# A two-layer decode kernel: W2's last blocks loaded over its first, more of head 29 kept, x on ScalarE's queue, and one small load in eight pieces

## The chip, the cores and the metric

The kernel runs on one core of a Trainium2 chip. The metric is device time in microseconds (us), and the time given for a kernel is the median of several executions. A profile is one execution taken by the hardware profiler. Its engines are PE (TensorE), DVE (VectorE), ACT (ScalarE), POOL (GpSimd) and SP (SyncE). Loads are issued by SP or ACT and carried out by sixteen DMA engines.

## The reference

One token passes twice through the same attention block and the same MLP. The cache does not change, so each layer reads all of it: 32 heads of 8192 keys and values of 128 numbers, in float32.

```
def _A_ref(x, k_cache, v_cache, wq, wo):
    q = (x @ wq).reshape(B, Sq, H, Dh).transpose(0, 2, 1, 3)      # H = 32, Dh = 128, D = 640
    scores = einsum("bhqd,bhkd->bhqk", q, k_cache) * (Dh ** -0.5) # Sk = 8192
    o = einsum("bhqk,bhkd->bhqd", softmax(scores), v_cache)
    return o.transpose(0, 2, 1, 3).reshape(B, Sq, H * Dh) @ wo
def _B_ref(x, w1, w2):                                            # Dff = 1728
    return relu(x @ w1) @ w2
x = x + _A_ref(layernorm(x), k_cache, v_cache, wq, wo)
x = x + _B_ref(layernorm(x), w1, w2)
x = x + _A_ref(layernorm(x), k_cache, v_cache, wq, wo)
x = x + _B_ref(layernorm(x), w1, w2)
```

## The kernel before

**Heads.** `attention_and_mlp` (L612) runs once per layer. Layer 1 (L = 0 in the code) takes heads 0 to 31, layer 2 (L = 1) takes them from 31 down to 0. For a head, `scores` (L443) multiplies the keys that lie in SBUF by the query; `row_maxima` and `exponentials` (L458, L461) make the softmax's numerators with DVE and ACT and turn them; `values` (L491) multiplies them by the values; `output` (L507) collects the head's column for the projection with `wo`. The last head of a layer is interleaved with the projection and the MLP (`before_last`, L662).

**The ring.** Keys, values and W2 lie in one large tile, `ring`. Its places are counted in units of 8 columns of all 128 partitions (4096 bytes). The table `UNITS` (L42 to L61) cuts each head into loads; a piece ("k", [(r, c, n)]) is n columns of keys of row r from column c on, a piece ("v", [(b, r, m)]) is a share of the values' block b. A load's pieces lie next to each other in memory, in the order of the table. `pump` (L190) issues loads from the list `todo` on SP's queue as long as the next one finds room, and `release` (L222) gives back a piece's place when TensorE has used it and pumps again. So SP's loads stand in the order of `todo`, and each waits for the reads that free its place.

**What is kept.** From the end of layer 1 some units stay in SBUF for layer 2, which takes these heads first: `DROPPED` (L62) says from which unit on, `KEPT` (L63) how many places they take. Two more pieces of head 30 (432 and 160 columns of keys) are loaded at the change of layers into tiles that layer 1 no longer needs, `mix` and `wct`, by `load_beside` (L210), called at L806 and L845. `pieces_of` (L227) takes the kept pieces of a head first in layer 2.

**W2.** W2's twelve full blocks (80 places each) come in four loads, `W2_RUNS` (L93: blocks 0 to 3, 4 to 7, 8 and 9, 10 and 11), and have 960 places of their own behind the kept ones at the end of layer 1. The loop at L859 reads them in the order 0 to 3, two short blocks that lie elsewhere, 4 to 11.

**Mixing.** At the ninth head of a layer (`where == 8`, L697) ACT loads one head's rows of `wo` (128 x 640) into `mix`; later steps multiply them by W1 beside the attention, so that the last head's output can go to the MLP directly. Just ahead of it on ACT's queue stands a load of Wq (`load_wq`, L239).

**Signals.** Each load signals one of eight semaphores, named DMAHW0 to DMAHW7 in the rows below, in turn over both queues; a load waits until the previous load on its own semaphore has landed. PE stands for TensorE's semaphore.

**The start.** SP issues x (L248), the first Wq (L249) and then the ring's loads.

Of the kernel before, what the change touches and what calls it, by code (L numbers as in the profile page):

```python
# [15 lines left out]
P = 128  # L16
D = 640
# [3 lines left out]
DFF = 1728  # L21
EPS = 1e-5
NB = D // P
HG = 4
# [21 lines left out]
UNITS[29] = [  # L46
    ("k", K_ALL[:1]),
    ("k", K_ALL[1:2]),
    ("k", [(2, 0, 512), (3, 0, 384)]),
    ("v", V_ALL[:1]),  # L50
    ("v", V_ALL[1:2]),
    ("k", [(3, 384, 128)]),
    ("v", V_ALL[2:3]),
    ("v", V_ALL[3:]),
]
UNITS[30] = [
    ("k", [(0, 432, 80), (1, 0, 80)]),
# [1 line left out]
    ("k", [(1, 80, 432)] + K_ALL[2:]),  # L59
] + HALVES[2:]  # L60
UNITS[31] = HALVES[:2] + LAST  # L61
DROPPED = {30: 2}  # L62
KEPT = 3800  # L63
MIX_AT = [12, 16, 20, 24]
AHEAD = 3

# [10 lines left out]
def wide(kind, piece):  # L77

    if kind == "w":
        return D // 8  # L80
    return 4 * piece[2] * (1 if kind == "k" else DH) // 8


def size(unit):
    return sum(wide(kind_of(unit, t), piece) for t, piece in enumerate(unit[1]))
# [4 lines left out]
F_TILES = 3  # L90
# [2 lines left out]
W2_RUNS = [range(0, 4), range(4, 8), range(8, 10), range(10, 12)]  # L93
UNITS["w2"] = [("w", list(run)) for run in W2_RUNS]
W2_ALL = [("w2", i) for i in range(len(W2_RUNS))]
RING = KEPT + 4 * F_TILES * D // 8


@with_exitstack
def decode_kernel(ctx: ExitStack, tc: tile.TileContext, x, kv, wq, wo, w1, w2, w2_rest, out):  # L100
    nc = tc.nc
# [11 lines left out]

    ring = consts.tile([P, 8 * RING], F32, name="ring")
    order = [(h, i) for h in range(H) for i in range(len(UNITS[h]))]
    kept = [u for u in order if u[0] >= min(DROPPED) and u[1] >= DROPPED.get(u[0], 0)]
    assert sum(size(UNITS[h][i]) for h, i in kept) == KEPT
    beside = [(1, u) for u in order if u[0] == 30 and u not in kept]
    todo = []

    def all_of(layer, u):
# [35 lines left out]
    for us, dram in ((order, kv), (W2_ALL, w2)):  # L157
        o = 0
        for u in us:
            n = 8 * P * size(UNITS[u[0]][u[1]])  # L160
# [5 lines left out]
    def place(layer, u, n):  # L166

        step = 512 if n % 512 == 0 else 8
        if layer:
            low, high = 0, RING  # L170
        elif u[0] in range(FULL[0]):
            low, high = 0, 16 * SLOT
        elif u[0] == "w2":
            low, high = KEPT, RING
        else:
            low, high = (3072, KEPT) if n == KEPT - 3072 else (0, 3072)
        at, best = low, None
        for a, m in sorted(live.values()) + [(high, 0)]:
            a = min(a, high)
            for base in (0, KEPT):  # L180
                c = base + -(-max(at - base, 0) // step) * step
                if a - c >= n and (best is None or a - at < best[1]):
                    best = c, a - at
            at = max(at, a + m)
        return None if best is None else best[0]
# [4 lines left out]
    def pump():  # L190
        while todo:
            layer, u, first, last, at = todo[0]
            unit = UNITS[u[0]][u[1]]
            ns = [wide(kind_of(unit, t), piece) for t, piece in enumerate(unit[1])]
            n = sum(ns[first:last])
            if at is None:
                at = place(layer, u, n)
                if at is None:
                    return
            elif not is_free(at, n):  # L200
                return
            todo.pop(0)
            o = 8 * sum(ns[:first])
            nc.sync.dma_start(ring[:, 8 * at : 8 * (at + n)], source[u][:, o : o + 8 * n])
            for t in range(first, last):
                live[layer, u, t] = at, ns[t]
                at_of[layer, u, t] = ring, 8 * at
                at += ns[t]

    def load_beside(where, at, n):  # L210
        layer, u = beside.pop()
        kind, pieces = UNITS[u[0]][u[1]]
        assert 8 * size(UNITS[u[0]][u[1]]) == n
        nc.sync.dma_start(where[:, at : at + n], source[u])
        for t, piece in enumerate(pieces):
            at_of[layer, u, t] = where, at
            at += 8 * wide(kind, piece)

    def key(L, u, t):
        return (0 if u in kept else L), u, t  # L220

    def release(L, u, t):  # L222
        if (L or u not in kept) and at_of[key(L, u, t)][0] is ring:
            del live[key(L, u, t)]
            pump()
# [13 lines left out]
    def load_wq(g, queue):  # L239
        wq_t[g] = wts.tile([P, NB, HG * DH], F32, name="wq_t")  # L240
        queue.dma_start(wq_t[g], wq[g])
# [3 lines left out]
        queue.dma_start(wo_t[g], wo[g])  # L245

    xr = work.tile([P, DR], F32, name="xr", bufs=2)
    nc.sync.dma_start(xr, x)  # L248
    load_wq(0, nc.sync)  # L249
    pump()  # L250
    load_wo(0, nc.sync)
# [24 lines left out]
    mix = consts.tile([P, DFF], F32, name="mix")  # L276
# [335 lines left out]
    def attention_and_mlp(L, xr, s):  # L612
        heads = list(range(H))[:: 1 - 2 * L]
        last = heads[-1]
# [35 lines left out]
        def run_out(k):  # L650

            projected(acc, runs[k], o_cols[k], k == 0, False)
            yield "dve"
            load_wo(groups[k + 1], nc.scalar)
# [26 lines left out]
        def due(h):  # L681

            where = heads.index(h)
            k, j = divmod(where, HG)
            if j == 0:
                o_cols[k] = work.tile([P, HG], F32, name="o_cols", bufs=2)
            if where and j == 0:
                chores.append([run_out(k - 1), "pe"])
            if j == 2 and k + 1 < NG:
                slow.append([queries_of(k + 1), "pe"])  # L690
            if where == H - 2:
                chores.append([first_of_last(), "pe"])
            if L == 0 and where == 4:
                nc.scalar.dma_start(w1_t, w1)
            if L == 0 and where == 7:
                nc.scalar.dma_start(w2_t, w2_rest)
            if where == 8:  # L697
                nc.scalar.dma_start(mix[:, :D], wo[last // HG][:, last % HG])
            if where == 11:
                slow.append([mixing(), "dve"])  # L700
            if where in MIX_AT:
                slow.append([mixing_quarter(MIX_AT.index(where)), "pe"])
# [20 lines left out]
        for where, h in enumerate(heads[:-1]):  # L723
# [36 lines left out]
            k, j = divmod(where, HG)  # L760
# [36 lines left out]
        rows = copied_rows(hd)  # L797
# [4 lines left out]

        xp, ph = mlp_in
        hidden(ph, o, mix, False, True)
        if L == 0:
            load_beside(mix, 0, DFF)  # L806
        pd = ps_m.tile([P, 512], F32, name="pm")
        times_rows(pd, wo_t[last // HG][:, last % HG], o, True, True)
        keep_busy(1, 128)
# [50 lines left out]
        for a, b in enumerate(blocks):  # L860
            if a == 2:
                ss = deviations(x1, s1)
            if a == 8:
                r1 = spread_of_rows(ss)
            rows = 2 * half if b == nb + 1 else P
            if b < nb:
                i = next(i for i, run in enumerate(W2_RUNS) if b in run)
                where = L, ("w2", i), b - W2_RUNS[i][0]
                tile_of, at = at_of[where]
                wt = tile_of[:, at : at + D]  # L870
            else:
                wt = w2_t[:rows, b - nb]
            times_rows(po, wt, hT[:rows, b : b + 1], a == 0, a == len(blocks) - 1)
            if b < nb:
                release(*where)

        x2 = work.tile([P, DR], F32, name="xr", bufs=2)
        s2 = work.tile([P, 1], F32, name="x_s", bufs=2)
# [7 lines left out]
    for L in range(2):  # L886
        xr, s = attention_and_mlp(L, xr, s)
# [80 lines left out]
```

## Time and profile before

| what | value |
|---|---|
| median of three runs (1351.44, 1353.2, 1356.7) | 1353.2 us |
| the profiled execution | 1351.49 us |
| its span, first to last instruction | 1349.7 us |
| moved | 575.17 MB, 426 GB/s over the span |
| SP's queue / ACT's queue | 531.89 MB / 42.44 MB |
| busy: PE / DVE / ACT | 59% / 19% / 4% of the span |

A timeline row reads: start, duration, engine, line, operation, output tile <- inputs, shapes, and in brackets the idle time of that engine before it with what ended it. SPq and ACTq rows are issues of loads. A row of the list of transfers ends with the size of one and the time from issue to landing (where neither stands, it was not recorded). A row of the windows gives start:end, length, the busy time of PE, PE's weight loads, DVE, ACT and POOL with their instruction counts, the clock granted to TensorE, the mean busy share of the sixteen DMA engines and their GB/s. The chain of waits is the work that ended last, followed back: start, length, what.

### The profile page before, as it was taken

Reading aid. Unit: us, or ns where it says so; the run is one execution under the profiler, and the core shown is the slowest. Engines: PE = TensorE matmul, PEld = TensorE weight load, DVE = VectorE, ACT = ScalarE, POOL = GpSimd, SP = SyncE. Lnnn points to the kernel's source line nnn. Section 1 sums busy time; section 2 is a strip of 40 time slices with the busy share of each in tenths; the row PEclk is TensorE's granted clock in tenths of the full one; section 3 lists DMA queues with packets and bytes.
Section 4 is the critical chain, followed back from the end, with each engine's and each line's share of the span. In section 5 each row is a group of like instructions: output and inputs, shape, how many; then the busy total and the mean of one; then the engine's idle time right before and its main releaser. Section 6 shows DMA issues by size and latency. Waiting matters only on the chain.

```text
span 1349.7 us, 13544 instructions
## 1 busy us (share of the span) xinstructions
PE 799.3 (59%) x6048; PEld 270.4 (20%) x6048; DVE 251.4 (19%) x794; ACT 59.2 (4%) x149; POOL 2.9 (0%) x10
## 2 busy tenths in 40 slices
PE   5455555554654655457787754555566554656658
PEld 2011111211211211122242211111121121212214
DVE  1111111221211211122122211122111211111212
ACT  0000000000000000000000000000000000000000
POOL 0000000000000000000000000000000000000000
PEclk8777677878978976788799777797778778777879
DMA  9999999999999999999999999999999999999997
GB/s 392 445 419 437 432 428 441 417 431 436 439 426 432 430 435 422 448 417 420 425 405 423 435 431 432 432 431 436 438 434 424 421 435 443 429 420 438 429 418 322
DMA packets 24977, 575.17 MB, mean 426 GB/s; under 512 B 2772, under 2 KB 2904, under 8 KB 5336
## 3 DMA queue, kind: packets, MB, share of 16 engines
q1 hardware_dynamic: 20312, 531.89, 91.8%
q10 hardware_dynamic: 4608, 42.44, 7.5%
q8 instruction: 47, 0.77, 0.2%
q14 instruction: 10, 0.08, 0.0%
HBM read 574.31 MB, written 0.00 MB: 426 GB/s over the span
## 4 chain that ended last, share of the span: by engine, by line
DMA 65%; PE 27%; DVE 5%; issue 1%; ACT 1%; ACTq 0%; SPq 0%; DVEq 0%
DMA ring<-in_kv 64%; PE ps L448 13%; PE outs L497 8%; DVE h_t L459 2%; PE px L387 1%; DVE pt L477 1%; PE pm L464 1%; ACT p L473 1%; DMA wo_t<-in_wo 1%; DVE p L516 1%; PE acc L419 1%; PE px L419 1%; PE acc L603 0%; PE px L590 0%; DVE pT L479 0%
## 5 line engine op out<-in xcount | busy, mean ns | idle before, releaser
L448 PE MATMUL ps<-ring,spread_q 128*32 128x512 f32 (+2 forms) x2072 | 331.0, 787 | 334.5 <-DMA ring<-in_kv 329.6
L497 PE MATMUL outs<-ring,pT 128*4 128x512 f32 (+1 forms) x2080 | 268.2, 658 | 27.7 <-DVE pT L479 17.4
L448 PEld LDWEIGHTS ps<-ring,spread_q 128*32 128x32 f32 x2072 | 76.9, 138 | 523.2 <-issue 298.4
L459 DVE TENSOR_REDUCE h_t<-ps 128x1 f32<-128x512 f32 x64 | 44.3, 692 | 640.3 <-PE ps L448 640.3
L473 ACT ACTIVATE p<-ps,h_t 128x512 f32<-128x512 f32 x64 | 44.0, 687 | 1226.4 <-DVE h_t L471 1226.4
L497 PEld LDWEIGHTS outs<-ring,pT 128*4 128x4 f32 x2080 | 52.5, 92 | 184.4 <-issue 156.9
L526 PE MATMUL pm<-ones,p 128*128 128x1 f32 x120 | 22.9, 260 | 94.8 <-DVE p L516 94.8
L512 DVE TENSOR_SCALAR p<-outs,ind 128x128 f32<-128x128 f32 x60 | 21.1, 351 | 248.2 <-PE outs L497 248.2
L516 DVE SCALAR_TENSOR_TENSOR p<-outs,ind,p 128x128 f32<-128x128 f32 x180 | 63.1, 351 | 6.4
L477 DVE STREAM_TRANSPOSE pt<-p 128x512 f32<-128x512 f32 x64 | 46.5, 727 | 57.9 <-ACT p L473 57.9
L464 PE MATMUL pm<-row_of,h_t 128*128 128x16 f32 x128 | 25.7, 276 | 49.9 <-DVE h_t L459 49.0
L526 PEld LDWEIGHTS pm<-ones,p 128*128 128x128 f32 x120 | 17.8, 188 | 151.5 <-DVE p L516 149.9
L464 PEld LDWEIGHTS pm<-row_of,h_t 128*128 128x128 f32 x128 | 19.4, 190 | 109.2 <-DVE h_t L459 107.3
L590 PE MATMUL px<-w_t,wct 128*128 128x448 f32 (+1 forms) x80 | 36.6, 573 | 1.1 <-ACT wct L583 1.1
L387 PE MATMUL px<-wq_t,ln_xc 128*32 128x256 f32 x280 | 32.9, 381 | 0.0
L486 PE MATMUL pm<-ind,h_t 128*128 128x1 f32 x128 | 23.4, 252 | 15.3 <-ACT p L473 15.3
L486 PEld LDWEIGHTS pm<-ind,h_t 128*128 128x128 f32 x128 | 23.2, 207 | 34.1 <-ACT p L473 26.6
L419 PE MATMUL acc<-wo_t,o_cols 128*32 128x160 f32 x496 | 22.7, 324 | 0.6 <-DVE o_cols L544 0.6
L527 DVE TENSOR_SCALAR o_cols<-pm,h_t 128x1 f32<-128x1 f32 x60 | 13.1, 218 | 30.6 <-PE pm L526 30.6
L387 PEld LDWEIGHTS px<-wq_t,ln_xc 128*32 128x32 f32 x280 | 15.2, 109 | 12.7 <-issue 1.2
L471 DVE TENSOR_REDUCE h_t<-pm 128x1 f32<-128x16 f32 x64 | 11.2, 175 | 32.4 <-PE pm L464 32.4
L419 PEld LDWEIGHTS acc<-wo_t,o_cols 128*32 128x32 f32 x496 | 15.8, 117 | 4.8 <-issue 2.5
(110 smaller groups left out, 201.2 us busy)
## 6 DMA issues: line engine op xcount, KB each, us to landing
ring<-in_kv SPq DMA_DIRECT2D x20, 4096.0 KB, 34.5
ring<-in_kv SPq DMA_DIRECT2D x38, 2048.0 KB, 29.3
ring<-in_kv SPq DMA_DIRECT2D x11, 6144.0 KB, 38.2
wq_t<-in_wq ACTq DMA_DIRECT2D x14, 1280.0 KB, 23.4
wo_t<-in_wo ACTq DMA_DIRECT2D x14, 1280.0 KB, 23.8
ring<-in_kv SPq DMA_DIRECT2D x15, 1024.0 KB, 16.7
ring<-in_w SPq DMA_DIRECT2D x4, 1280.0 KB, 26.8
w_t<-in_w ACTq DMA_DIRECT2D x1, 4320.0 KB, 47.7
```

The lines of the kernel that those rows point to most:

```text
L387: nc.tensor.matmul(pq[32 * j : 32 * j + 32, :n], xc[:, c : c + 1].to_broadcast([P, 32]), wq_t[g][:, c, j * n : (j + 1) * n], start=(c == 0 ...
L419: nc.tensor.matmul(acc[32 * g : 32 * g + 32, :DR], col.to_broadcast([col.shape[0], 32]), wt[:, g * DR : (g + 1) * DR], start=first, stop=last,
L448: nc.tensor.matmul(hd.ps[32 * g : 32 * g + 32, c : c + n], spread_q[:, 3 - r : 35 - r], tile_of[:, at + g * n : at + (g + 1) * n], start=f ...
L459: nc.vector.tensor_reduce(hd.nm, hd.ps, AX.X, ALU.max, negate=True)
L464: nc.tensor.matmul(pt[:, :16], hd.nm.to_broadcast([P, P]), row_of.rearrange("p g r -> p (g r)"), start=True, stop=True,)
L473: nc.scalar.activation(hd.p, hd.ps, AF.Exp, bias=hd.low, scale=1.0, accum_out=hd.l)
L477: nc.vector.transpose(pt, hd.p)
L486: nc.tensor.matmul(pt[:, :1], hd.l.to_broadcast([P, P]), ind[:, 4:5], start=True, stop=True)
L497: nc.tensor.matmul(hd.out[32 * g : 32 * g + 4, r : r + m].rearrange("p r d -> p (r d)"), hd.pT[:, 4 * i : 4 * i + 4], tile_of[:, v : v + m ...
L516: nc.vector.scalar_tensor_tensor(oc[:, r], hd.out[:, r], ind[:, r : r + 1], oc[:, r - 1], op0=ALU.mult, op1=ALU.add,)
L526: nc.tensor.matmul(pt[:, :1], oc[:, 3], ones, start=True, stop=True)
L590: nc.tensor.matmul(pt[:, :n], wct[:, c], w1_t[:, c, f : f + n], start=(c == 0), stop=(c == NB - 1),)
```

## The change

Four things are changed, with what follows from them.

- W2 gets 800 places instead of 960 in layer 1. Its last load (blocks 10 and 11) is placed over blocks 0 and 1, once these have been read. The load into `wct` now comes ahead of it, and the load into `mix` follows it.
- The 160 places go to 320 columns of keys of head 29, as one more unit at the end of its list. Head 29's keys are cut anew, so that their parts fit the places: seven pieces instead of five.
- x is issued by ACT instead of SP.
- In layer 2 the 128 rows of `wo` for mixing are loaded by eight loads of 96, 11, 6, 5, 4, 3, 2 and 1 rows.

```
 UNITS[29] = [
     ("k", K_ALL[:1]),
     ("k", K_ALL[1:2]),
-    ("k", [(2, 0, 512), (3, 0, 384)]),
+    ("k", [(2, 0, 256)]),
+    ("k", [(2, 256, 256), (3, 128, 64)]),
     ("v", V_ALL[:1]),
     ("v", V_ALL[1:2]),
-    ("k", [(3, 384, 128)]),
+    ("k", [(3, 0, 128)]),
     ("v", V_ALL[2:3]),
     ("v", V_ALL[3:]),
+    ("k", [(3, 192, 320)]),
 ]
...
-DROPPED = {30: 2}
-KEPT = 3800
+MIX_CUT = [[P], [96, 11, 6, 5, 4, 3, 2, 1]]
+DROPPED = {29: 9, 30: 2}
+KEPT = 3960
+W2_PLACES = 800
...
-RING = KEPT + 4 * F_TILES * D // 8
+RING = KEPT + W2_PLACES
...
-    beside = [(1, u) for u in order if u[0] == 30 and u not in kept]
+    apart = {(29, 9): (3800, KEPT), (30, 0): (4464, 4544), (30, 1): (4544, RING), (30, 2): (3072, 3800)}
+    beside = [(1, u) for u in order[::-1] if u[0] == 30 and u not in kept]
...
+        elif u in apart:
+            low, high = apart[u]
         else:
-            low, high = (3072, KEPT) if n == KEPT - 3072 else (0, 3072)
+            low, high = 0, 3072
...
-            for base in (0, KEPT):
+            for base in (0, 3328, KEPT):
...
-    nc.sync.dma_start(xr, x)
+    nc.scalar.dma_start(xr, x)
...
             if where == 8:
-                nc.scalar.dma_start(mix[:, :D], wo[last // HG][:, last % HG])
+                p = 0
+                for rows in MIX_CUT[L]:
+                    part = slice(p, p + rows)
+                    nc.scalar.dma_start(mix[part, :D], wo[last // HG][part, last % HG])
+                    p += rows
...
         hidden(ph, o, mix, False, True)
-        if L == 0:
-            load_beside(mix, 0, DFF)
...
             if b < nb:
                 release(*where)
+            if L == 0 and a == 1:
+                load_beside(mix, 0, DFF)
```

Three places show how instructions moved. The first is TensorE in layer 1: the values of head 28, its output, head 29's scores (ps<-ring), then head 29's softmax and values. Before:

```order
L497 MATMUL outs_118<-ring,pT 4x512 x16
L526 MATMUL pm<-ones,p 128x1
L448 MATMUL ps<-ring,spread_q 32x512 x12
L448 MATMUL ps<-ring,spread_q 32x384 x4
L448 MATMUL ps<-ring,spread_q 32x128 x4
L464 MATMUL pm<-row_of,h_t 128x16
```

Of the change:

```order
L504 MATMUL outs_118<-ring,pT 4x512 x16
L533 MATMUL pm<-ones,p 128x1
L455 MATMUL ps<-ring,spread_q 32x512 x8
L455 MATMUL ps<-ring,spread_q 32x256 x8
L455 MATMUL ps<-ring,spread_q 32x64 x4
L455 MATMUL ps<-ring,spread_q 32x128 x4
L455 MATMUL ps<-ring,spread_q 32x320 x4
L471 MATMUL pm<-row_of,h_t 128x16
```

The last piece of the scores was the 128 columns that are loaded between the values; now it is the 320 columns, loaded after all of head 29's values.

The second place is SP's queue at the change of layers, with the semaphores that each load waits for; in_w is W2, the loads into mix and wct are head 30's keys, and the ring's loads behind them are head 29's for layer 2. Before:

```order
L204 DMA ring<-in_w 128x2560 [waits DMAHW1_49]
L204 DMA ring<-in_w 128x2560 [waits DMAHW2_49]
L204 DMA ring<-in_w 128x1280 [waits DMAHW3_49]
L204 DMA ring<-in_w 128x1280 [waits DMAHW4_49]
L214 DMA mix<-in_kv 128x1728 [waits DVE_49,DMAHW5_49,PE_49,Activation_49]
L214 DMA wct<-in_kv 128x640 [waits DVE_49,DMAHW6_49,PE_49,Activation_49]
L204 DMA ring<-in_kv 128x2048 [waits DMAHW7_49,DMAHW1_49,PE_49]
```

Of the change:

```order
L211 DMA ring<-in_w 128x2560 [waits DMAHW3_49]
L211 DMA ring<-in_w 128x2560 [waits DMAHW4_49,PE_49]
L211 DMA ring<-in_w 128x1280 [waits DMAHW5_49,PE_49]
L221 DMA wct<-in_kv 128x640 [waits DVE_49,DMAHW6_49,PE_49,Activation_49]
L211 DMA ring<-in_w 128x1280 [waits DMAHW7_49,DMAHW3_49,PE_49]
L221 DMA mix<-in_kv 128x1728 [waits DMAHW0_49]
L211 DMA ring<-in_kv 128x2048 [waits DMAHW4_49,DMAHW1_49,PE_49]
```

W2's fourth load and the load into mix now stand behind the load into wct, which waits for the last matmuls that read wct.

The third place is the mixing load of layer 2. On ACT's queue stand the load of Wq, the mixing rows and the exponentials of head 23 (the ninth head of the layer) and then of later heads. Before:

```order
L241 DMA wq_t<-in_wq 128x2560 [waits DMAHW7_49,DMAHW0_49]
L698 DMA mix<-in_wo 128x640 [waits DMAHW5_49,DMAHW0_49]
L473 ACTIVATE p,h_t<-ps,h_t 128x512 [waits DVE_49,Activation_49]
L245 DMA wo_t<-in_wo 128x2560 [waits DMAHW2_49,PE_49]
L473 ACTIVATE p,h_t<-ps,h_t 128x512 [waits DVE_49,Activation_49] x3
```

Of the change:

```order
L248 DMA wq_t<-in_wq 128x2560 [waits DMAHW4_49,DMAHW2_49]
L708 DMA mix<-in_wo 96x640 [waits DMAHW3_49,DMAHW0_49]
L708 DMA mix<-in_wo 11x640 [waits DMAHW4_49]
L708 DMA mix<-in_wo 6x640 [waits DMAHW5_49]
L708 DMA mix<-in_wo 5x640 [waits DMAHW6_49]
L708 DMA mix<-in_wo 4x640 [waits DMAHW7_49]
L708 DMA mix<-in_wo 3x640 [waits DMAHW0_49]
L708 DMA mix<-in_wo 2x640 [waits DMAHW1_49]
L708 DMA mix<-in_wo 1x640 [waits DMAHW2_49]
L480 ACTIVATE p,h_t<-ps,h_t 128x512 [waits DVE_49,Activation_49]
```

On SP's queue at the same time stand the loads of heads 24 (whole), 23 (in two loads), 22 (whole) and 21 (its first two). Before:

```order
L204 DMA ring<-in_kv 128x16384 [waits DMAHW1_49,DMAHW0_49,PE_49]
L204 DMA ring<-in_kv 128x4096 [waits PE_49]
L204 DMA ring<-in_kv 128x12288 [waits DMAHW3_49,DMAHW2_49,PE_49]
L204 DMA ring<-in_kv 128x16384 [waits DMAHW4_49,PE_49]
L204 DMA ring<-in_kv 128x8192 [waits DMAHW5_49,PE_49]
```

Of the change:

```order
L211 DMA ring<-in_kv 128x16384 [waits DMAHW4_49,DMAHW7_49,DMAHW1_49,PE_49]
L211 DMA ring<-in_kv 128x4096
L211 DMA ring<-in_kv 128x12288 [waits DMAHW6_49,DMAHW5_49,PE_49]
L211 DMA ring<-in_kv 128x16384 [waits DMAHW7_49,DMAHW3_49,PE_49]
L211 DMA ring<-in_kv 128x8192 [waits DMAHW5_49,DMAHW0_49,PE_49]
```

Head 22's load now waits for DMAHW3, which the piece of 96 rows on ACT's queue signals; the piece of one row waits for DMAHW2, which Wq ahead of it signals.

## The prediction

> **What bounds the kernel now.** I read the page's chain and DMA rows first, then the list of transfers, then windows and timelines where the change acts. The whole cache goes through once per layer, and the chain that ended last is mostly the arrival of keys and values.
>
> ```profile
> span 1349.7 us, 13544 instructions
> DMA packets 24977, 575.17 MB, mean 426 GB/s; under 512 B 2772, under 2 KB 2904, under 8 KB 5336
> DMA 65%; PE 27%; DVE 5%; issue 1%; ACT 1%; ACTq 0%; SPq 0%; DVEq 0%
> ```
>
> Transfers hold 65% of that chain; the PE share is largely its last stretch, where arithmetic follows the last long arrival without a pause:
>
> ```profile
> 1266.60 28.68 DMA ring<-in_kv
> 1295.28 0.04 issue
> 1295.32 5.26 PE ps L448 x32
> ```
>
> From 1295.28 to the end, 54.4 us, the chain names no transfer. So whatever brings that arrival (head 2) forward brings the end forward by as much, provided that the loads behind it, the last of them W2's, move with it. At the end the sixteen DMA engines do not finish together. The columns that count here are the last two, DMA share and GB/s:
>
> ```profile
> 1339.00:1340.00 1.00, 1.00 (x18) 0.53 (x10) 0.41 (x1) 0.00 (x0) 0.00 (x0) 1.00 0.71 292
> 1341.00:1342.00 1.00, 0.97 (x24) 0.70 (x24) 0.56 (x5) 0.00 (x0) 0.00 (x0) 1.00 0.48 200
> 1344.00:1345.00 1.00, 1.00 (x30) 0.72 (x22) 0.16 (x1) 0.00 (x0) 0.00 (x0) 1.00 0.11 46
> ```
>
> The share sinks over 6 us instead of falling at once: some engines are done by 1339, others work until 1345. A load has landed when its last engine has, so a gap costs time only where it leaves the late engines idle.
>
> **Fewer bytes.** 160 more places of head 29 stay in the ring. A place is 8 columns of 128 partitions of 4 bytes, 4096 bytes; 160 are 0.655 MB that layer 2 no longer reads. At 426 GB/s that is 1.54 us, all of it on the path if the queue never runs dry: **-1.5**. Half of it is the least I would believe (-0.8), if the missing load leaves a hole in the queue when layer 2 begins.
>
> **x on ScalarE's queue.** SyncE issues x and then the first Wq; TensorE waits for the latter.
>
> ```profile
> 0.74 0.39 SPq L248 DMA_DIRECT2D xr<-in_x  x1
> 1.19 0.41 SPq L241 DMA_DIRECT2D wq_t<-in_wq  x1
> 6.75 2.36 PE L364 MATMUL px<-wq_t,ln_xc 128*32 128x128 f32 x40 [1.29 <-DMA wq_t<-in_wq]
> 9.18 0.38 ACTq L241 DMA_DIRECT2D wq_t<-in_wq  x1
> ```
>
> Every SyncE load moves up by 1.19 - 0.74 = 0.45 us. ScalarE's first work is at 9.18, so x delays nothing there. The bytes of x still pass through the same engines, so it may be nothing; the start is all transfers, hence **-0.4**, from 0 to -0.45. Should x land a little later, 1.29 us of waiting for Wq cover it.
>
> **The end of layer 1.** The kept piece of head 29 is now the last of its loads, so its scores end later. The last key piece that head 29 waited for, the load after its last values (320 KB, the second of two issued from 638.74, at 639.2, landing 14.4 later), and the two waits that follow on TensorE:
>
> ```profile
> 638.74 0.85 SPq L204 DMA_DIRECT2D ring<-in_kv  x2
> ring<-in_kv SPq DMA_DIRECT2D x1, 320.0 KB, 14.4
> 647.83 0.65 PE L448 MATMUL ps<-ring,spread_q 128*32 128x128 f32 x8 [3.28 <-DMA ring<-in_kv]
> 662.74 4.24 PE L448 MATMUL ps<-ring,spread_q 128*32 128x432 f32 x24 [2.71 <-DMA ring<-in_kv]
> 682.37 1.92 PE L448 MATMUL ps<-ring,spread_q 128*32 128x512 f32 x16 [0.94 <-DMA ring<-in_kv]
> ```
>
> The bytes up to that 320 KB load are the same in both kernels, so the kept piece lands where head 29's last values did: 639.2 + 14.4 = 653.6, less 0.8 for 320 KB at 426 GB/s, is 652.8. Its 320 columns take about 0.85 (0.65 for 128 columns here). Scores end at 653.7 instead of 648.5: 5.2 later. Head 30's wait gives back 2.71 and the last head's 0.94, so layer 1's arithmetic ends 5.2 - 2.71 - 0.94 = 1.55 later against the transfers. That is hidden unless SyncE's queue runs dry, and here it can:
>
> ```profile
> 677.44 5.23 SPq L204 DMA_DIRECT2D ring<-in_w  x2
> ring<-in_w SPq DMA_DIRECT2D x1, 640.0 KB, 22.6
> 695.90 0.33 SPq L214 DMA_DIRECT2D mix<-in_kv  x1
> 697.82 0.33 SPq L214 DMA_DIRECT2D wct<-in_kv  x1
> 700.96 1.84 PE L419 MATMUL px<-ring,hT 128*32 128x160 f32 x48
> ```
>
> Of W2's four loads the last now stands behind the load into wct, so SyncE issues nothing between 677.4 and the time at which wct is free, 697.82 before and 697.82 + 1.55 = 699.4 now. The third W2 load lands at 677.44 + 22.6 = 700.0. Its late engines stop shortly before 700.0, and the next data begin shortly after 699.4:
>
> ```profile
> wq_t<-in_wq SPq DMA_DIRECT2D x1, 1280.0 KB, 5.5
> xr<-in_x SPq DMA_DIRECT2D x1, 80.0 KB, 2.0
> ```
>
> x (last row, from issue to landing), issued to idle engines, took 2.0 to land, 0.2 of it transfer: up to 1.8 of delay. The late engines idle for between nothing and 699.4 + 1.8 - 700.0 = 1.2, or 1.6 if the end of the data lies 0.4 ahead of the landing. I take **+0.5**, nearer to the low end, because part of the 1.8 is the signal at the end, which a following load does not wait for. TensorE should not wait for the late W2 blocks: it reaches the fifth of the six blocks of the 700.96 row at 700.96 + 4 x 0.31 + 1.55 = 703.7, when wct and the last W2 load (0.96 MB, 2.3 us) have followed on 700.5. Behind come the same loads as before, less 0.655 MB. The windows there, share and rate last:
>
> ```profile
> 695.00:700.00 5.00, 4.88 (x86) 3.19 (x80) 2.16 (x12) 0.37 (x2) 0.00 (x0) 1.00 0.96 371
> 700.00:705.00 5.00, 4.10 (x84) 3.17 (x80) 1.11 (x7) 0.00 (x0) 0.56 (x1) 1.00 0.97 356
> 705.00:710.00 5.00, 4.38 (x66) 2.60 (x70) 0.85 (x4) 0.00 (x0) 0.55 (x1) 1.00 1.03 432
> ```
>
> The engines were busy even at 705 to 710, when layer 2's first releases are still to come; 1.5 us less in the queue should not empty it, and if it does, that is the hole of the first term.
>
> **The mixing load in eight.** In layer 2 ScalarE issued Wq and the mixing rows right after an exponential and was then idle:
>
> ```profile
> 840.18 0.69 ACT L473 ACTIVATE p<-ps,h_t 128x512 f32<-128x512 f32 x1 [29.24 <-DVE h_t L471]
> 840.28 0.33 ACTq L241 DMA_DIRECT2D wq_t<-in_wq  x1
> 840.71 0.39 ACTq L698 DMA_DIRECT2D mix<-in_wo  x1
> 857.69 0.69 ACT L473 ACTIVATE p<-ps,h_t 128x512 f32<-128x512 f32 x1 [16.73 <-DVE h_t L471]
> wq_t<-in_wq ACTq DMA_DIRECT2D x1, 1280.0 KB, 24.3
> mix<-in_wo ACTq DMA_DIRECT2D x1, 320.0 KB, 39.1
> 845.68 0.33 SPq L204 DMA_DIRECT2D ring<-in_kv  x1
> 853.75 2.41 PE L448 MATMUL ps<-ring,spread_q 128*32 128x512 f32 x16 [0.37 <-DMA ring<-in_kv]
> 874.89 5.50 PE L448 MATMUL ps<-ring,spread_q 128*32 128x512 f32 x32 [9.72 <-DMA ring<-in_kv]
> ```
>
> Seven more issues of about 0.4 us are 3 us out of 16.73 idle: nothing. The waits matter. All loads share eight signals in turn, and each waits for the previous load on its own signal. Eight pieces use up all eight. So the next SyncE load, head 22's (issued at 845.68, needed at 874.89), must wait for the first piece, 96 rows behind all of Wq, and ScalarE's eighth piece for Wq itself; behind that one stands the exponential of 857.69. SyncE's queue then ends with the load that landed at 853.7. By then Wq has had 13.4 of its 24.3 us, so some 45% of 1.31 MB is left, 1.4 us at 426 GB/s, and the 96 rows take 0.6: the piece lands near 855.7. ScalarE is free at about 856, ahead of 857.69; were it 7 us later, the 9.72 of idle time before 874.89 would still hold it. But head 22's load is issued at 855.7 with nothing before it, and the engines idle until it starts, at most 1.8 by the row of x. In the other direction, up to 1.9 more (3.7 in all) if Wq is further back than the straight line says, nothing if other rows are left over on the late engines. I take **+1.2**, nearest to the row of x less its closing signal.
>
> Read literally, 39.1 us from issue to landing would put the piece near 880. [...]
>
> [...]
>
> **Sum.** -1.5 - 0.4 + 0.5 + 1.2 = -0.2. The profiled execution lasted 1351.5 (span 1349.7 and 1.8 around it); by the sum it becomes 1351.3. The three runs shown have their median at 1353.2, 1.7 higher, so I predict **1353.0**. About 0.5%, 6.8 us, is what a measurement of this kernel can tell from no change.
>
> **Rivals.** *Both gaps are covered* (0.18): the late engines never idle, only the savings remain, -1.9, 1351.3. For it: a DMA share of about 1.0 nearly everywhere. Against it: the waits are in the program's order. *Both gaps at their upper bounds* (0.09): -1.9 + 1.6 + 3.7 = +3.4, 1356.6. For it: the change of layers already runs below rate (share 0.96, 371 GB/s, from 695).
>
> *Slower: the first mixing piece holds SyncE* (0.03): if ScalarE's queue is not sped up by an empty neighbour, the piece lands at 879.8, the engines lie idle from 853.7 but for 1.9 us of Wq and rows, 24.2 in all, and the end moves by 24.2 - 1.9 + 0.5 = 22.8: 1376. It decides once the piece lands more than 8 us after 855.7 (6.8 and the 1.4 that the rest gains). Against it stands the 5.5 of the first Wq. The forecast itself has 0.70.
>
> **The numbers.** Faster by over 0.5% would need 6.8 us, and all savings are 1.9: 0.01. Slower by over 0.5%: the last rival and a remainder, 0.04. Same: 0.95. The range takes in the covered case with the scatter of the runs below their median (1.8), 1349.5, and both upper bounds, 1356.6.
>
> **What would show it.** 574.5 MB moved; a Wq landing 0.4 earlier at the start; head 29's scores in layer 1 ending after its values have landed; a dip of the DMA share near 700; in layer 2 SyncE's load of head 22 issued about 10 us later than the row of 845.68, right after the first mixing piece, with a dip of 1 to 2 us in the share and TensorE's wait at 874.89 longer by as much. Wrong would be: that load issued on time, a ScalarE exponential late by more than 10 us, or an end that differs by more than 4 us.

## The result and the profile after

The changed kernel takes 1357.86 us (median of 22 runs, 1354.08 to 1361.05), the kernel before in the same session 1354.24 (22 runs). The ratio is 1.0029, 95% interval [1.0020, 1.0038]: 3.9 us slower (2.7 to 5.1), where the sum had -0.2. The measured time lies 1.3 above the upper end of the predicted range. Of this, 1.0 is the base, which had been 1353.2 over three runs. The profiled execution took 1357.78 (before 1351.49). Its page:

```profile
span 1356.0 us, 13627 instructions
GB/s 395 440 426 433 431 435 431 431 425 436 435 427 425 443 429 424 440 418 421 428 358 425 430 437 434 357 446 434 422 433 432 426 432 439 432 420 441 430 419 326
DMA packets 25441, 574.52 MB, mean 424 GB/s; under 512 B 2852, under 2 KB 2984, under 8 KB 6056
DMA 64%; PE 28%; DVE 5%; issue 1%; ACT 1%; ACTq 0%; another core or an unknown queue 0%; SPq 0%; DVEq 0%
```

The 0.65 MB are saved. In the row of 40 slices two stand out, the 21st (678 to 712 us) with 358 and the 26th (848 to 881) with 357 GB/s: the two places that the prediction named. The end is bound by transfers as before.

**The change of layers.** SyncE's issues, and the windows (the last three columns are the clock granted to TensorE, the DMA share and GB/s):

```profile
698.30 0.33 SPq L221 DMA_DIRECT2D wct<-in_kv  x1
699.40 0.33 SPq L211 DMA_DIRECT2D ring<-in_w  x1
699.78 0.42 SPq L221 DMA_DIRECT2D mix<-in_kv  x1
```
```profile
695.00:700.00 5.00, 4.68 (x54) 3.31 (x58) 1.62 (x10) 0.37 (x2) 0.00 (x0) 0.77 0.58 209
700.00:705.00 5.00, 5.00 (x66) 2.87 (x62) 0.84 (x5) 0.00 (x0) 0.55 (x1) 0.50 0.92 324
705.00:710.00 5.00, 4.23 (x56) 2.77 (x52) 0.96 (x7) 0.00 (x0) 0.00 (x0) 0.70 0.91 329
```

The share falls to 0.58 before the load into wct starts. Against the 371, 356 and 432 GB/s of before, 1.49 MB are missing, 3.5 us at 426 GB/s. Part of it seems to go with the clock, 0.50 where before had 1.00: the run with the small load whole, at 1.00 until 705, misses 0.66 MB (below).

**The mixing load.** A piece of the chain that ended last, and ScalarE, TensorE and windows of 1 us there:

```profile
841.76 16.93 DMA mix<-in_wo
858.70 0.02 SPq L211
858.72 0.03 issue
858.75 24.20 DMA ring<-in_kv
```
```profile
842.19 16.27 ACTq L708 DMA_DIRECT2D mix<-in_wo  x7
862.02 0.69 ACT L480 ACTIVATE p<-ps,h_t 128x512 f32<-128x512 f32 x1 [20.02 <-DVE h_t L478]
883.09 6.49 PE L455 MATMUL ps<-ring,spread_q 128*32 128x512 f32 x32 [12.76 <-DMA ring<-in_kv]
```
```profile
854.00:855.00 1.00, 0.00 (x0) 0.00 (x0) 0.00 (x0) 0.00 (x0) 0.00 (x0) 0.87 0.71 156
855.00:856.00 1.00, 0.00 (x0) 0.00 (x0) 0.00 (x0) 0.00 (x0) 0.00 (x0) 0.50 0.42 149
856.00:857.00 1.00, 0.35 (x4) 0.20 (x8) 0.00 (x0) 0.00 (x0) 0.00 (x0) 0.50 0.38 125
857.00:858.00 1.00, 1.00 (x8) 0.20 (x4) 0.00 (x0) 0.00 (x0) 0.00 (x0) 0.50 0.11 44
858.00:859.00 1.00, 1.00 (x8) 0.20 (x4) 0.00 (x0) 0.00 (x0) 0.00 (x0) 0.50 0.02 8
```

The chain runs through the small load itself: head 22's load is issued at 858.75, 0.05 after the first piece (96 rows) has landed. That is 3.0 later than the predicted 855.7, but the load of SyncE just before it lands at 856.61 here: the piece lands 2.1 behind it, where the prediction had 2.0. The share, though, does not drop at once. It sinks from 0.71 to 0.02 over 5 us, because the sixteen engines finish one after another (the piece's sixteen landings lie between 854.72 and 858.70). The new load's first packets begin at 859.7. Worked out from the packets, from 854 until all engines work again the mean of the sixteen is idle for 3.8 us. From the landing at 858.70 to the first packets the latest engine idles 1.0, close to the +1.2 of the sum; the rest of the 3.8 is idle time of the engines that were through earlier.

The landings tell where time was lost. Head 24's load lands at 834.49 (before 832.35): 2.1 late, the change of layers. Head 2's lands at 1301.27 (before 1295.28) and W2's last at 1350.60 (before 1345.05): another 3.4 to 3.8 behind the change of layers, where the mixing load is the one place that stands out. At the end the engines finish closer together, and the share sinks over 4 us instead of 6:

```profile
1345.00:1346.00 1.00, 1.00 (x16) 0.40 (x16) 0.02 (x1) 0.00 (x0) 0.00 (x0) 1.00 1.03 425
1347.00:1348.00 1.00, 0.88 (x23) 0.80 (x26) 0.47 (x5) 0.00 (x0) 0.00 (x0) 1.00 0.60 251
1349.00:1350.00 1.00, 1.00 (x32) 0.56 (x22) 0.64 (x3) 0.00 (x0) 0.00 (x0) 1.00 0.46 180
```

W2's last load lands with a spread of 3.66 us between its engines (before 5.43). That is the first sign that the engines were brought level somewhere, and the experiments follow it.

### The profile page after: what moved, and what is told of

The parts are those of the page before. It is cut to its first block, busy times and chain, and to the rows that moved or that the text cites. A ratio compares the mean times of both kernels' runs of the same rounds, so it can differ in the third digit from the quotient of the medians.

```text
span 1356.0 us, 13627 instructions
## 1 busy us (share of the span) xinstructions
PE 794.4 (59%) x6080; PEld 272.2 (20%) x6080; DVE 251.7 (19%) x794; ACT 59.1 (4%) x149; POOL 2.9 (0%) x10
## 4 chain that ended last, share of the span: by engine, by line
DMA 64%; PE 28%; DVE 5%; issue 1%; ACT 1%; ACTq 0%; another core or an unknown queue 0%; SPq 0%; DVEq 0%
DMA ring<-in_kv 63%; PE ps L455 13%; PE outs L504 8%; DVE h_t L466 2%; PE px L394 1%; DMA mix<-in_wo 1%; DVE pt L484 1%; PE pm L471 1%; ACT p L480 1%; PE px L426 1%; DVE p L523 1%; PE acc L426 0%; PE acc L610 0%; PE px L409 0%; DVE pT L486 0%
## 5 line engine op out<-in xcount | busy, mean ns | idle before, releaser
L455 PE MATMUL ps<-ring,spread_q 128*32 128x512 f32 (+3 forms) x2104 | 326.4, 768 | 338.9 <-DMA ring<-in_kv 333.5
L504 PE MATMUL outs<-ring,pT 128*4 128x512 f32 (+1 forms) x2080 | 261.7, 645 | 31.4 <-DVE pT L486 16.3
L426 PEld LDWEIGHTS acc<-wo_t,o_cols 128*32 128x32 f32 x496 | 16.1, 121 | 5.0 <-issue 2.2
```

Of the source, the lines that this page charges most:

```text
L426: nc.tensor.matmul(acc[32 * g : 32 * g + 32, :DR], col.to_broadcast([col.shape[0], 32]), wt[:, g * DR : (g + 1) * DR], start=first, stop=last,
L455: nc.tensor.matmul(hd.ps[32 * g : 32 * g + 32, c : c + n], spread_q[:, 3 - r : 35 - r], tile_of[:, at + g * n : at + (g + 1) * n], start=f ...
L504: nc.tensor.matmul(hd.out[32 * g : 32 * g + 4, r : r + m].rearrange("p r d -> p (r d)"), hd.pT[:, 4 * i : 4 * i + 4], tile_of[:, v : v + m ...
```

## The experiments

Single times of one kernel lie up to 8.5 us apart, so medians are compared, by the ratio to the kernel before in the same session (median 1353.0 to 1354.5) with its 95% interval. 0.1% is 1.35 us.

### Which part costs: one part at a time

The changed kernel with the small load whole:

```
-MIX_CUT = [[P], [96, 11, 6, 5, 4, 3, 2, 1]]
+MIX_CUT = [[P], [P]]
```

> The changed kernel with the small wo load of layer 2 whole again (one load of 320 KB). Theory (two gaps in the transfers cost about 2.7 us at the change of layers and 3.4 us in layer 2, against 1.9 us saved): the second gap goes, 848 to 860 us runs at full rate again, ScalarE waits no longer before the exponential of head 23; the time falls by 3.4 us against the changed kernel and ends 0.8 us above before, ratio 1.0006 (1.000 to 1.0015). Rival A (the late scores of head 29 and the later start of layer 2 carry the loss through TensorE, the division costs nothing): it stays at the changed kernel's 1.0029. Rival B (the gap at the change of layers is absorbed by later waits): 1.9 us faster than before, ratio 0.9986.

Measured: 1.0003 [0.9994, 1.0011], as the theory had it.

```profile
695.00:700.00 5.00, 4.80 (x82) 3.31 (x82) 2.18 (x13) 0.37 (x2) 0.00 (x0) 1.00 0.59 222
700.00:705.00 5.00, 4.01 (x87) 2.81 (x79) 0.55 (x3) 0.00 (x0) 0.56 (x1) 1.00 1.01 390
705.00:710.00 5.00, 4.50 (x49) 3.11 (x49) 1.37 (x8) 0.00 (x0) 0.55 (x1) 0.66 1.00 415
850.00:860.00 10.00, 6.12 (x50) 2.48 (x50) 1.59 (x3) 0.78 (x2) 0.00 (x0) 0.60 1.04 449
```

The second dip is gone (449 GB/s). The first stays, though TensorE's clock is 1.00 until 705: 222, 390 and 415 against 371, 356 and 432 are 0.66 MB, 1.5 us. That is what the smaller number of bytes was to bring (0.655 MB).

The kernel before with nothing but the division in eight (the loop over `MIX_CUT` from the change):

> The kernel before with nothing but the small wo load of layer 2 divided in eight. Theory: head 22's load is issued only after the first piece of 96 rows has landed, some 13 us late, the engines lie idle for about 3.4 us near 855, and the end moves by 3.4 us: ratio 1.0025 (1.0015 to 1.0035). Rival A (the division costs nothing): ratio 1.000. [...]

Measured: 1.0029 [1.0018, 1.0040]. The whole loss of the change comes with this part alone. The windows of this run, and below them that of before from 850 to 860:

```profile
840.00:850.00 10.00, 7.05 (x34) 1.52 (x34) 2.51 (x9) 0.78 (x2) 0.00 (x0) 0.66 0.97 419
850.00:860.00 10.00, 7.77 (x54) 2.24 (x58) 1.25 (x4) 0.20 (x1) 0.00 (x0) 0.66 0.71 240
860.00:870.00 10.00, 6.65 (x60) 1.82 (x48) 2.72 (x9) 0.58 (x2) 0.00 (x0) 0.83 1.05 452
```
```profile
850.00:860.00 10.00, 7.97 (x78) 2.99 (x82) 2.34 (x8) 0.78 (x2) 0.00 (x0) 0.83 1.04 448
```

The kernel before with nothing but x on ScalarE's queue (`nc.scalar.dma_start(xr, x)`):

> The kernel before with nothing but x issued on ScalarE's queue. Theory as recorded: every load of SyncE is issued 0.4 us earlier at the start, and the end comes 0.4 us earlier: ratio 0.9997 (0.999 to 1.0003), by time alone hardly to be told from nothing; in the trace the first Wq is issued near 0.75 instead of 1.19 us and lands 0.4 us earlier. Rival: x on the other queue lands later and holds TensorE's first work, or the first loads share the engines with x: no gain, Wq lands at the same time.

Measured: 1.0004 [0.9992, 1.0015], no difference; the time alone could not tell -0.4 from nothing, but the trace can. The list of transfers and TensorE's first work with Wq:

```profile
wq_t<-in_wq SPq DMA_DIRECT2D x1, 1280.0 KB, 6.0
xr<-in_x ACTq DMA_DIRECT2D x1, 80.0 KB, 6.2
```
```profile
9.56 2.36 PE L364 MATMUL px<-wq_t,ln_xc 128*32 128x128 f32 x40
```

Wq is issued at 0.74 instead of 1.19, but takes 6.0 instead of 5.5 and lands at 6.72 (before 6.71). x, now beside Wq, lands at 6.89 instead of 2.73, and TensorE starts with it at 9.56 instead of 6.75. The rival held: the two loads share the engines. The later start of TensorE does not show in the transfers: the first load of the ring lands at 11.63, before at 11.60.

### What a dry queue costs

The prediction counted only what the latest engine idles. Four drains of SyncE's queue, in the kernel before:

```
+    landed = consts.tile([1, 32], F32, name="landed")
...
+            if layer and u[0] in (20, 16, 12, 8) and first == 0:
+                nc.sync.dma_start(landed, ring[:1, 8 * at : 8 * at + 32])
```

> The kernel before with four tiny loads of 128 bytes on SyncE, each reading the data of the load just issued, for heads 20, 16, 12 and 8 of layer 2. SyncE waits there until that load has landed on all sixteen engines before it issues the next, so its queue runs dry four times and nothing else changes. Restarting costs about 1.8 us each time. The prediction's rule (only the latest engine's idle time counts): 4 x 1.8 = 7.2 us, ratio 1.0053 (1.004 to 1.0065). Theory now (each time the lead of the earlier engines, on average 1.8 us ahead of the latest, is lost and builds up again): 13 us, ratio 1.0095 (1.007 to 1.012), and the spread of the landings is under 1 us behind each.

Measured: 1.0119 [1.0103, 1.0134], 16.1 us, 4.0 for each drain (in the traces W2's last load lands at 1360.94, before at 1345.05). The prediction's rule, with its 7.2 us, is out. The four drains in numbers worked out from the trace's packets and landings, in us: mean lead is how long the sixteen engines had finished, on average, when the last one did; the gap runs from that last landing to the next load's first packets, on average; the last column is by how much the first row of each engine took longer than the rows behind it.

```
drained at   spread   mean lead   gap    first rows longer by
  916.81      3.70      1.73      2.05        0.66
 1004.94      1.70      1.05      1.95        0.70
 1083.67      2.00      1.53      2.05        0.57
 1182.17      1.70      1.31      1.94        0.65
```

The sum is 16.2. Gap and slow first rows alone, all that the latest engine loses, are 10.6 (1.0078), under the interval. The lead of the others is lost as well, because the engines start nearly level and then fall apart anew (why, in the last section). Of that, 1.7 comes back at the end, where W2's last load has a mean lead of 1.06 instead of 2.74: 14.5, within the interval (13.9 to 18.1).

The change of layers alone, the loads into wct and mix in the order of the change, with W2 in its own places:

```
-    beside = [(1, u) for u in order if u[0] == 30 and u not in kept]
+    beside = [(1, u) for u in order[::-1] if u[0] == 30 and u not in kept]
...
-        if L == 0:
-            load_beside(mix, 0, DFF)
...
+            if L == 0 and a == 1:
+                load_beside(mix, 0, DFF)
```

> The kernel before with the loads of head 30's first two pieces at the change of layers in the order of the change: the one into wct first, the one into mix only behind W2's first two blocks. W2 keeps its own places, so nothing but SyncE's idle time before 697.8 is added. The latest engines have W2's last load until 701.5, the earliest seven are through at 696.5 to 697.5. The prediction's rule (only the latest engine's idle time counts): nothing, ratio 1.000. Theory (mean idle time): seven engines by 2.5 us, 1.1 us, ratio 1.0008 (1.000 to 1.0016); in the trace the DMA share from 695 to 700 falls to about 0.75 and the spread behind it to under 3 us, in either case.

Measured: 1.0011 [1.0001, 1.0021], as the mean of the engines has it; the interval leaves out the rule's 1.000 only just.

```profile
695.00:700.00 5.00, 4.42 (x57) 3.20 (x57) 1.67 (x10) 0.74 (x3) 0.00 (x0) 1.00 0.66 275
700.00:705.00 5.00, 4.47 (x100) 3.27 (x100) 1.33 (x7) 0.00 (x0) 0.55 (x1) 1.00 0.90 330
```

The latest engines had W2's last load until 701.63. Still the share falls to 0.66, and the spread of the landings from 5.28 (that load) to 1.05 (wct, the next).

The change with the load into mix ahead again, and the small load whole:

> The changed kernel with the small wo load whole, and with the load into mix issued again right after the last use of the wo rows, ahead of the load into wct, as in the kernel before (head 30's two parts go out in the order of before). Theory (idle engines at the change of layers): the load of 0.88 MB fills the hole between 697 and 702, the dip from 695 to 710 shrinks from 2.7 us to under 1.3 us, and the time is 1.4 to 2.7 us below the run with the whole load in the order of the change, so 0.6 to 1.9 us below before: ratio 0.9986 to 0.9996. Rival (TensorE's wait for the last W2 load is what costs): that load stands behind 0.88 MB more, lands up to 2 us later, layer 2 starts later by as much, and the time is equal to or up to 2 us above the other run: ratio 1.0006 to 1.002.

Measured: 1.0004 [0.9994, 1.0013], the same as with the order of the change (1.0003). The time does not decide between the two, and the 1.5 that the hole was to cost did not come back.

```profile
695.00:700.00 5.00, 4.88 (x86) 3.25 (x82) 2.16 (x12) 0.37 (x2) 0.00 (x0) 1.00 0.86 316
710.00:715.00 5.00, 4.54 (x36) 1.97 (x32) 0.69 (x3) 0.00 (x0) 0.00 (x0) 0.50 0.93 348
715.00:720.00 5.00, 4.07 (x38) 1.06 (x34) 0.92 (x3) 0.00 (x0) 0.00 (x0) 0.92 0.93 340
```

The hole shrinks as the theory wanted (0.86 instead of 0.59), but in this execution TensorE ran at half clock from 705 to 715, and the share falls to 0.93 from 710 to 720. That late releases of places are the reason was not shown.

### What the pieces cost beside the dry queue

Five pieces leave three of the eight signals free (in the kernel before, `[96, 14, 9, 5, 4]`):

> The kernel before with the small wo load of layer 2 in five pieces (96, 14, 9, 5 and 4 rows). Head 22's load then shares its signal with a load that landed long before, is issued near 845.7 as in before, and only the load after it waits, for Wq, while head 22's 8.4 MB keep the engines busy. Theory (the loss comes from SyncE's queue running dry behind the first piece): ratio 1.000 (0.999 to 1.001), no dip between 850 and 860. Rival A (small pieces cost by themselves, on the engines that carry them): still two thirds of the loss of the division in eight, ratio 1.002.

Measured: 1.0015 [1.0003, 1.0027]. No dip between 850 and 860, head 22's load issued at 845.69, and yet slower: my theory was short of something, and rival A stood up. Six pieces (`[96, 11, 9, 5, 4, 3]`):

> The kernel before with the small wo load of layer 2 in six pieces (96, 11, 9, 5, 4 and 3 rows). Head 22's load then waits for the landing of the SyncE load just before it, near 853.7, 2.7 us earlier than in the division in eight; Wq on ScalarE's queue keeps the late engines busy until near 856. The prediction's rule (a gap costs only what the latest engine idles): the latest engine has work until the new data come near 855.4, ratio 1.000. Theory now (all engines are brought level, so the mean idle time of the sixteen counts): 853.8 on average to 855.4, 1.6 us and no more than 2.5, ratio 1.0012 (1.0005 to 1.002); the spread of the sixteen engines falls from 4 us to under 2.5 us behind it.

Measured: 1.0027 [1.0016, 1.0039], more than either had. Head 22's load went out at 858.63, 0.07 after the landing it waits for, which in this execution came at 858.56. Its first rows took 3.12 us instead of 2.42: these 0.7 were not in the theory. The eight pieces two heads earlier (`where == 6`):

> The kernel before with the division in eight, issued two heads earlier in layer 2, where neither Wq nor SyncE's last queued load stands in front. All eight pieces are as in the change. ScalarE is held for some 15 to 20 us, which its idle time of 19 us between two exponentials covers nearly, and SyncE keeps two loads in its queue. Theory: ratio 1.000 (0.9993 to 1.001), no dip of the DMA share. Rival A (the small pieces cost by themselves): ratio 1.0029 as for the division in its place.

Measured: 1.0023 [1.0014, 1.0033], but for a reason that I had excluded:

```profile
808.10 1.30 SPq L206 DMA_DIRECT2D ring<-in_kv  x3
```
```profile
800.00:810.00 10.00, 2.37 (x14) 0.98 (x18) 1.60 (x5) 0.00 (x0) 0.00 (x0) 0.73 0.68 235
```

SyncE's next load waited for the piece of 11 rows (landed 808.05), and the queue ran dry here too. So the eight signals do it at both places, and this run doesn't judge rival A. The run with five pieces does. In its trace the rows of the ring's loads, which otherwise nearly always take the same time to within 1%, were slower from Wq's landing until the last piece's, without exception until 880: rows of 64 KB 2.5 to 3.0 us instead of 2.42. Two runs separate the number of pieces from their shape. Two pieces of rows (`[96, 32]`):

> The kernel before with the small wo load of layer 2 in two pieces, 96 and 32 rows. No signal runs short, head 22's load is issued near 845.7 as in before. In the run with five pieces each row of 64 KB took 2.5 to 2.9 us instead of 2.42 from the time at which the piece of 96 rows began. Theory B (a piece whose rows aren't eight to an engine slows all engines while it is under way): rows of 64 and 32 KB take 5 to 10% longer for some 16 us behind Wq, 1.0 to 1.5 us in all, ratio 1.001 (1.0003 to 1.0017). Rival D (the number of loads under way at once slows them): two loads, rows at 2.42 and 1.22 us throughout, ratio 1.000.

Measured: 1.0024 [1.0012, 1.0036]. Rival D is out; theory B has the right sign, but its 1.001 (up to 1.0017) is small. In the trace the loads land 2.8 us later than before already ahead of the pieces, from the change of layers (its clock there is in the last section), and 4.8 behind them: the slow rows cost 2.0, where the theory had 1.0 to 1.5. Five pieces of columns:

```
-                nc.scalar.dma_start(mix[:, :D], wo[last // HG][:, last % HG])
+                wide_by = [D, D // 5][L]
+                for c in range(0, D, wide_by):
+                    nc.scalar.dma_start(mix[:, c : c + wide_by], wo[last // HG][:, last % HG, c : c + wide_by])
```

> The kernel before with the small wo load of layer 2 in five pieces again, but each of all 128 rows and 128 of the 640 columns, so that each engine has eight rows of each piece as in the whole load. Theory B (rows that aren't eight to an engine slow all engines): rows of 64 KB keep their 2.42 us, ratio 1.000 (0.9992 to 1.0008). Rival D (the number of loads under way): the same loss as with five pieces of rows, ratio 1.0015, rows of 64 KB at 2.5 to 2.9 us between 864 and 890.

Measured: 0.9992 [0.9981, 1.0002]. The same stretch in the run with 96 and 32 rows, in that with five pieces of columns, and before:

```profile
870.00:880.00 10.00, 1.05 (x8) 0.45 (x12) 0.00 (x0) 0.00 (x0) 0.00 (x0) 0.50 0.96 361
880.00:890.00 10.00, 7.42 (x55) 2.09 (x48) 1.96 (x6) 0.78 (x2) 0.00 (x0) 0.84 0.96 396
```
```profile
870.00:880.00 10.00, 4.91 (x32) 1.32 (x32) 0.00 (x0) 0.00 (x0) 0.00 (x0) 0.61 0.95 405
880.00:890.00 10.00, 6.13 (x40) 1.60 (x36) 3.07 (x10) 0.78 (x2) 0.00 (x0) 0.83 1.01 426
```
```profile
870.00:880.00 10.00, 5.11 (x32) 1.40 (x32) 0.00 (x0) 0.00 (x0) 0.00 (x0) 0.57 0.94 403
```

At a share of 0.96 the engines move 361 GB/s with two pieces of rows and 405 (share 0.95) with five of columns: busy, but slower. The rows, from the packets of the trace, between 866 and 880:

```
                       64 KB rows      32 KB rows
96 and 32 rows         2694 ns (x51)   1406 ns (x50)
five pieces of columns 2425 ns (x55)   1222 ns (x214), 864 to 890
before, steady         2422 ns         1217 ns
```

So it is the shape, not the number. While the pieces of 96 and 32 rows were under way, six and two rows to an engine on average instead of eight, every row of 64 KB was slower (2.60 us or more). Which property of the shape does it stays open.

Eight pieces of columns (128 x 80), with the waits of the eight and without their shape:

> The kernel before with the small wo load of layer 2 in eight pieces of all 128 rows and 80 columns. The waits are those of the division in eight rows: head 22's load waits for the first piece, the eighth piece for Wq. Theory: the drained queue alone costs about 3 us (restart 1.9 us behind the last landing, 0.7 us for slow first rows, mean lead of the earlier engines 1.5 us, less what Wq fills), ratio 1.002 (1.0012 to 1.003), with a dip between 850 and 860 and a spread under 1 us behind it. Rival (the loss of the division in eight comes mostly from the uneven rows): ratio under 1.001.

Measured: 1.0028 [1.0015, 1.0041], within the theory's range and not the rival's.

```profile
850.00:860.00 10.00, 8.14 (x78) 3.07 (x82) 2.21 (x8) 0.78 (x2) 0.00 (x0) 0.83 0.91 326
860.00:870.00 10.00, 3.39 (x30) 0.84 (x22) 1.62 (x5) 0.00 (x0) 0.00 (x0) 0.92 0.92 398
```

Without uneven rows the loss is the same. (Rows of 320 bytes cost a little themselves: 1024 of 22 ns against 128 of 104 ns in the whole load are 0.6 us for each engine.) The dry queue (0.28%) and the shape (0.24%) don't add up with the eight pieces of rows (0.29%). The packets say why: by the time that the eight pieces run, SyncE's queue is nearly empty, and few rows are there to be slowed. Worked out from the packets, the rows slowed beside the eight pieces come to 0.5 us for each engine, with 96 and 32 rows to 1.9.

## Why the prediction was wrong, point by point

**The step that failed** is the sentence "a gap costs time only where it leaves the late engines idle", and with it above all the term of the mixing load. It takes the lateness of an engine for a fixed property. In the drained kernel the landings lie 3.70 apart ahead of the first drain, those of fifteen engines within 0.82 behind it, and then the engines fall apart anew, so a lead that is given away is not had back. What counts is the mean idle time of all sixteen: four drains cost 16.1 us, where the idle time and the slow rows of the latest engine are 10.6. With the run of eight pieces of columns (1.0028, a dry queue without uneven rows) this is shown for the mixing load; for the change of layers the evidence is thinner.

**The mixing load, +1.2 (0 to 3.7).** The chain of events was right: the first piece holds SyncE's load, a dip, TensorE waiting 12.76 instead of 9.72. The price was not: 3.9 [2.4, 5.4] alone. The latest engine's idle time, the one thing that was priced, came out near the 1.2 (1.0). Missing were the leads of the earlier engines (Wq's sixteen landings lie 4.0 to 4.4 apart here, in the run with the division alone and in the changed kernel), which make it 3.8 in the profiled execution, and 0.7 for the slow first rows (3.11 us instead of 2.42). Some 1.1 of this comes back at the end, where W2's last load has a mean lead of 1.63 instead of 2.74: 3.4 in all. For the shape of the pieces the sum had nothing either; here it adds little, as eight pieces of columns cost the same. ScalarE's late eighth piece cost nothing, as said: its exponential at 862.02 waited for DVE.

The place of 855.7 rests on an estimate of the author, that Wq and the 96 rows move at the full 426 GB/s once SyncE's queue is empty; no run shows that rate there. In the changed kernel the windows show 125 and 44 GB/s from 856 to 858. What the traces show besides: where both queues had work, a row of the small load came between two rows of 64 KB (before, from the packets: 64 KB until 864.55, 2560 bytes until 864.65, 64 KB until 867.07), and the load landed 39.1 after its issue. In the changed kernel, with SyncE's queue running empty, the 96 rows landed 16.9 after theirs, in sixteen landings from 854.72 to 858.70; in the run with 96 and 32 rows, where the queue was full, 37.8.

**The change of layers, +0.5 (0 to 1.6).** The place was right. The size is 1.5 [0.1, 2.8] alone and 1.5 by the windows of the first experiment: three times the +0.5, though within its bounds, and the interval does not exclude the +0.5. Head 29's scores end after its values have landed, as said:

```profile
653.32 1.29 PE L455 MATMUL ps<-ring,spread_q 128*32 128x320 f32 x8 [5.89 <-DMA ring<-in_kv]
```

They end at 654.6, 6.1 later (predicted 5.2; the 320 columns took 1.29, not 0.85); but wct's load came only 0.5 later (698.30; predicted 1.55). So the wait that the sum counted hardly grew. The loss came from the load into mix, which no longer stands ahead of it at 695.9, and from the early engines, through at 695.2. TensorE did not wait for W2's last blocks, as said:

```profile
703.97 3.43 PE L426 MATMUL px<-ring,hT 128*32 128x160 f32 x48
```

**Fewer bytes, -1.5.** The bytes are gone. Without the division the changed kernel gains nothing (1.0003 [0.9994, 1.0011]). That the bytes gain 1.5 and the hole at the change of layers takes them back fits the windows, but the worth of the bytes alone was not measured.

**x, -0.4.** An earlier issue is not an earlier landing: Wq landed at 6.72 instead of 6.71, so nothing.

**The sum**, with what the runs showed: -1.5 (kept, not measured) + 0 + 1.5 + 3.9 = 3.9, and 3.9 was measured. Both gaps at their upper bounds was a rival with 0.09 and 1356.6. Its +3.4 lies within the measured 2.7 to 5.1, but by luck: it has the same rule, and its 3.7 for the mixing load stood for a Wq further back, while the piece landed where it was worked out, 2.1 behind SyncE's load. Of the three signs named for "wrong" one came out, in the profiled executions: an end 5.55 later than before. By the medians the end is 3.6 later.

## What to carry to other kernels

Where transfers bind, price a dry queue by all engines: the time from the last landing to the first new packets, the slow first rows, and the mean lead of the engines that were through early; here 4 us a time. Before a load is divided, count the signals that its pieces take from the loads behind them on either queue (five pieces of columns cost nothing here, eight 0.28%), and try a cut along the columns rather than the rows (two pieces of rows cost 0.24% here). The earlier issue gained nothing here, as the load then shared the engines with the one that it passed: Wq, issued 0.45 earlier, landed at 6.72 instead of 6.71.

## What the runs showed of the hardware

- Rows of one size take the same time nearly everywhere: 64 KB 2.42 us, 48 KB 1.82, 32 KB 1.22. A longer row is therefore a sign. After a drain the first rows of 64 KB took 2.7 to 3.5.
- Engines fall behind one at a time, by steps of 1 to 1.6 us: behind the first drain fifteen landings lie within 0.82 us, the sixteenth at 2.08; behind the fourth, 0.52 and 1.70. Behind the fourth drain each step comes with one packet of 16 KB of the queue that the profile calls instruction (first row below, drained kernel: packets, MB, share). The first such packet there starts at 1194.27; after one, two, three, four and five of them, one, two, three, four and five engines land more than 1 us behind the others. That the late engine is the one that carried the packet is inferred, as the records do not name engines.
- TensorE's clock at the change of layers differs between executions. With the 96 and 32 rows, a kernel that is the same as before up to 840, it was 0.50 there, and 319 GB/s were moved instead of 356; 48 multiplications of W2 take 3.43 us at it (after, above) and 1.84 at 1.00. Why it falls in some executions stays open. That window is the second row below.

```profile
q8 instruction: 47, 0.77, 0.2%
700.00:705.00 5.00, 5.00 (x62) 2.61 (x54) 0.79 (x4) 0.00 (x0) 0.00 (x0) 0.50 0.89 319
```
